# Grouped-query decode attention with an MLP: the query weights in two loads, the output weights in two pieces

## The chip, the cores and the metric

The kernel runs on one core of one Trainium2 chip. The metric is the device time of one execution in microseconds; the kernel before has a median of 1303.21 us over three runs.

## What is computed

One token goes through a layer norm; the normed row feeds an attention block with a cached key and value, and beside it a two-layer MLP; the sum of both and of the input is the output. All is float32.

```
x  = A_x                                   # 1 x 512
xn = layernorm(x)
q  = (xn @ wq) -> 32 heads of 128          # wq 512 x 4096
k, v: 8 heads of 65536 x 128, each shared by 4 query heads
p  = softmax(q k^T * 128**-0.5);  o = p v
out = x + (o -> 4096) @ wo + relu(xn @ w1) @ w2     # wo 4096 x 512, w1 512 x 1792, w2 1792 x 512
```

## The kernel before

The cache is 512 MB and is read once. Keys and values come in 64 chunks of 8 MB (32 of each), 128 rows (one per partition) of 64 KB each; the key chunk goes to the tile `kt`, the value chunk to `vt`, so each of the two is filled again as soon as its reader gives it free. There are four chunk pairs (PARTS) for each of 8 key heads.

The order is written out by hand on each engine, with named semaphores.

SyncE (SP) issues all the large loads, on one queue. First the query weights `wq` into `kt`, in the pieces of WQ_CUTS (floats per row; L151 for the first, L159 for the rest), then w1 into `wt` (L160), then key and value chunks in turn, each after the semaphore that frees its tile (L161 to L170). Behind the last value chunk come the output weights `wo` into `kt`, in the pieces of WO_CUTS (L171 to L173; a slice is 512 floats, 2 KB of a row, and there are 32), and, after `hT` is there, w2 into `wt` in five pieces (L175 to L177). The output is stored at L179.

TensorE (PE) turns through one loop NCH + 2 = 34 times (L270 to L322). The back half of each turn is "scores": eight rounds of 2048 columns of `kt`, four matmuls each (eight recorded passes each, since they are float32), against the padded query tile `qpad` (L307 to L320). Turn 0 uses it for `xn @ wq`, turns 1 to 32 for the key chunks, turn 33 for `o @ wo`: this is why both weights go to `kt`. Ahead of the rounds PE takes two semaphores: `q` (qpad is written) and `k` (16 counts of a landed load). The front half of a turn (from turn 2) is the maximum, the MLP's first product, probabilities times values (L292) and the row sums (L299, L302). Behind the last turn PE does w2 (L331, L339), the sum over the heads' parts (L328 with `yd`, L352 with `ysum`).

VectorE (DVE) transposes the scores out of PSUM, two rounds at a time into `tr` (turn_scores, L361 to L368), and raises `free` for PE behind each. PE's rounds 6 and 7 take four counts of `free`. In turns 0 and 33 the names in `gates` put a wait for a load into two of these four steps: a drain behind the transpose that waits for the load's 16 counts, and only then raises `free`. So rounds that read a later piece wait for that piece by way of DVE. In turn 33 DVE then reduces to yT, spreads it to `yd` (L409), adds `ysum` (L413) and transposes the result (L417).

GpSimd (POOL) finishes the layer norm (L208 to L212), takes `ends` (the landing of the first piece of wq), writes `xn` into `qpad` and raises `q` (L213, L214); later it does the MLP's first product's scaling (L219 to L224) and `hT` (L226).

The semaphores of wq's three pieces are `ends`, `k` and `wq2`; those of wo's three pieces `k`, `wo1` and `wo2`.

```
WQ_CUTS = [4096, 4096, 8192]
WQ_SEMS = ["ends", "k", "wq2"]
WO_CUTS = [16, 8, 8]
...
take(pe, sem("q"))
take(pe, sem("k"), 16)
for s in range(ROUNDS):
```

Of the kernel before, what the change touches and what calls it, by code (L numbers as in the profile page):

```python
# [37 lines left out]
XA = D // P  # L38
WIDE = 4
ROUNDS = 8  # L40
WQ_CUTS = [4096, 4096, 8192]
WQ_SEMS = ["ends", "k", "wq2"]
WO_CUTS = [16, 8, 8]
W2_CUTS = [6, 4, 2, 1, 1]
W2_SUM = 12
W2_ROWS = 10
# [3 lines left out]
def take(e, sem, n=1):  # L50

    return e.sem_inc(sem, -n).wait_op(sem, n, "sem-ge")  # L52


def starts(cuts):
    return [sum(cuts[:i]) for i in range(len(cuts) + 1)]
# [3 lines left out]
def attention_and_mlp_kernel(  # L60
# [12 lines left out]
    sp, pe, dve, act, pool = nc.sync, nc.tensor, nc.vector, nc.scalar, nc.gpsimd  # L73
# [7 lines left out]
    def sem(name):  # L81
        if name not in sems:
            sems[name] = nc.alloc_semaphore(name)
        return sems[name]

    def after(ins, name, n=1):

        return ins.wait_op(sem(name), n, "sem-ge")
# [53 lines left out]
    v_row = v[0].rearrange("(n p b) d -> n p (b d)", p=P, b=NB)  # L142
    wq_at, wo_at, w2_at = starts(WQ_CUTS), starts(WO_CUTS), starts(W2_CUTS)

# [5 lines left out]

    load = sp.dma_start(kt[:, : WQ_CUTS[0]], wq_row[:, : WQ_CUTS[0]]).then_inc(sem(WQ_SEMS[0]), 16)  # L151
    tc.no_tile_sem_insts.add(load.ins.name)
# [3 lines left out]
    inside = section.enter_context(tc.tile_critical(sync_engine=mybir.EngineType.Pool, no_gpsimd_drain=True))  # L156
    for i in range(1, len(WQ_CUTS)):
        cut = slice(wq_at[i], wq_at[i + 1])
        sp.dma_start(kt[:, cut], wq_row[:, cut]).then_inc(sem(WQ_SEMS[i]), 16)  # L159
    sp.dma_start(wt, w1_row).then_inc(sem("w1"), 16)  # L160
# [9 lines left out]
    take(sp, sem("kfree"))  # L170
    for i in range(len(WO_CUTS)):  # L171
        cut = slice(wo_at[i] * D, wo_at[i + 1] * D)
# [11 lines left out]
    def link(ins):  # L184

        if chain[0]:
            after(ins, "pool", chain[0])
        chain[0] += 1
        return ins.then_inc(sem("pool"), 1)
# [21 lines left out]
    link(pool.tensor_mul(st[:, 7:8], st[:, 5:6], st[:, 6:7]))  # L211
    link(pool.tensor_scalar_mul(xn, xc, st[:, 7:8]))  # L212
    take(pool, sem("ends"), 16)  # L213
    after(pool.tensor_copy(qpad[:, :XA], xn), "pool", chain[0]).then_inc(sem("q"), 1)  # L214
    f = DFF_ALL
    w1_of = [wt[:, a * f : (a + 1) * f] for a in range(XA)]
# [144 lines left out]
    def turn_scores(gates=(), free=None):  # L361

        for s in range(ROUNDS // 2):
            if free and s == ROUNDS // 2 - 1:
                after(dve.nop(), "p2d", s + 1).then_inc(sem(free), 1)
            ins = after(dve.transpose(tr2[:, s * 1024 : (s + 1) * 1024], pair[s % 2]), "p2d", s + 1)  # L366
            if s < len(gates):
                ins = after(dve.drain(), gates[s], 16)  # L368
            ins.then_inc(sem("free"), 1)

    dve.memset(ones, 1.0)
    dve.memset(banks, 0.0).then_inc(sem("zero"), 1)
    after(dve.reciprocal(st[:, 5:6], st[:, 4:5]), "ln", 3).then_inc(sem("ln"), 1)
    turn_scores(["wq2", "wq2"], free="kfree")
    dve.drain()
    dve.tensor_reduce(qall, of_own_row(NQ, XA), axis=AX.X, op=ALU.add).then_inc(sem("dve"), 1)
    take(dve, sem("p2d"), 4)
    take(dve, sem("dve"))
    with dve.Fori(0, HEADS) as h:
        dve.tensor_copy(qpad[:, :GROUP], qall[:, bass.ds(h * GROUP, GROUP)]).then_inc(sem("q"), PARTS)  # L380
        with dve.Fori(0, PARTS):
            turn_scores()
            dve.drain()
            dve.reduce_max(m, tr.rearrange("p b i -> p i b")[:, :GROUP, :], axis=AX.X).then_inc(sem("d2p"), 1)  # L384
            after(dve.reduce_max(mg, pma[:GROUP, :P], axis=AX.X), "p2d", 5).then_inc(sem("dve"), 1)
            after(
                dve.tensor_scalar(dg, ident[:GROUP, :GROUP], mg, -scale, op0=ALU.mult, op1=ALU.mult), "dve", 1  # L387
            ).then_inc(sem("d2p"), 1)
            after(dve.tensor_tensor(nb_new, pmb[:, :GROUP], nb_run, op=ALU.min), "p2d", 6).then_inc(sem("dve"), 1)
            after(dve.tensor_sub(diff, nb_new, nb_run), "dve", 2).then_inc(sem("dve"), 1)  # L390
            after(dve.tensor_copy(nb_run, nb_new), "dve", 3).then_inc(sem("bias"), 1)
            after(dve.tensor_copy(o_sb.rearrange("p b d -> p (b d)"), acc), "p2d", 7).then_inc(sem("d2p"), 1)  # L392
            dve.tensor_mul(lo_run, lo_run, corr).then_inc(sem("dve"), 1)
            take(dve, sem("p2d"), 8)
            after(dve.tensor_add(lo_run, lo_run, lo_new), "dve", 4).then_inc(sem("dve"), 1)  # L395
            take(dve, sem("dve"), 5)
        dve.reciprocal(diff, lo_run[:, 0, :]).then_inc(sem("dve"), 1)
        dve.memset(nb_run, 3.0e38)
        after(
            dve.tensor_mul(oT[:, bass.ds(h * GROUP, GROUP)], lo_run[:, 1, :], diff), "dve"  # L400
        ).then_inc(sem("dve"), 1)
        take(dve, sem("dve"), 2)
    dve.tensor_copy(qpad, oT).then_inc(sem("q"), 1)
    dve.transpose(ysum[:, : FB * 32], hrow).then_inc(sem("hx"), 1)  # L404
    turn_scores(["wo1", "wo2"])
    dve.drain()
    dve.tensor_reduce(yT, of_own_row(CT, NQ), axis=AX.X, op=ALU.add).then_inc(sem("dve"), 1)
    after(
# [2 lines left out]
        ), "dve",  # L411
    ).then_inc(sem("yd"), 1)
    after(dve.tensor_add(ysum, y4, x4), "p2d", 5).then_inc(sem("ysum"), 1)  # L413
    for _ in range(3):
        dve.drain()
    after(
        dve.transpose(ysb.rearrange("p i a -> p a i"), yacc.rearrange("p (e a) -> p a e", a=CT)), "p2d", 6  # L417
# [38 lines left out]
```

## Time and profile before

| | us |
|---|---|
| median of 3 runs (1303.2 to 1303.97) | 1303.21 |
| span of the profiled execution | 1301.3 |
| PE busy | 774.9 |
| DVE busy | 274.8 |
| ACT busy | 76.2 |
| POOL busy | 34.8 |
| HBM read | 560.99 MB, 431 GB/s over the span |

The profiled execution's span runs from its first to its last instruction; the median of the runs is 1.9 us longer, and that rest lies outside the span. Shares of busy time are averages: what counts for this change is the first 25 us and the last 35 us, so the timeline of these two stretches is read, with the issue and the landing of the loads.

### The profile page before, as it was taken

The page shows a single profiled execution, that of the slowest core. Times are in us where ns is not written, and L with a number is a line of the kernel's source. Part 1 is how long each engine was busy: PE and PEld are TensorE (multiplying, and loading weights), DVE is VectorE, ACT ScalarE, POOL GpSimd, SP SyncE. Part 2 cuts the span into 40 slices and gives each one's busy share as a digit, 9 for nine tenths or more (in the row PEclk, how much of TensorE's full clock was granted, in tenths as well). Part 3 has the DMA queues.
Part 4 walks back from the last instruction along what each step waited for, and adds up shares of the span by engine and source line. Part 5 has one row for each costly group of instructions (what it writes and reads, how often), then busy time and mean ns, then how long its engine had stood idle before and what let it go on. Part 6 is the DMA issues. An engine that isn't in the chain of part 4 may idle for free.

```text
span 1301.3 us, 13055 instructions
## 1 busy us (share of the span) xinstructions
PE 774.9 (60%) x5474; PEld 231.1 (18%) x5474; DVE 274.8 (21%) x466; ACT 76.2 (6%) x299; POOL 34.8 (3%) x30
## 2 busy tenths in 40 slices
PE   3365674665576456566555566666567466557557
PEld 1111121111121111121111121111112111112112
DVE  2211222211222220222220122221122221122222
ACT  1000000000000000000000000000000000000000
POOL 1900000000000000000000000000000000000000
PEclk9677877776887777786776777677777777777779
DMA  9999999999999999999999999999999999999998
GB/s 403 451 419 451 419 451 419 435 435 419 451 419 451 419 451 419 449 421 423 447 419 451 419 451 419 451 419 435 435 419 451 419 451 419 451 419 443 427 420 370
DMA packets 11236, 561.02 MB, mean 431 GB/s; under 512 B 1505, under 2 KB 1505, under 8 KB 1890
## 3 DMA queue, kind: packets, MB, share of 16 engines
q1 hardware_dynamic: 11088, 561.00, 99.7%
q10 hardware_dynamic: 146, 0.00, 0.0%
q8 instruction: 1, 0.02, 0.0%
q14 instruction: 1, 0.01, 0.0%
HBM read 560.99 MB, written 0.00 MB: 431 GB/s over the span
## 4 chain that ended last, share of the span: by engine, by line
issue 94%; DMA 3%; POOL 2%; SPq 0%; PE 0%; DVE 0%; POOLq 0%
DMA wt<-w 3%; POOL wt L219 1%; POOL wt L224 0%; POOL wt L222 0%; POOL wt L223 0%; SPq L177 0%; SPq L159 0%; PE banks L339 0%; DVE ysb L417 0%; SPq L151 0%; POOL hT L226 0%; SPq L452 0%; POOLq L156 0%
## 5 line engine op out<-in xcount | busy, mean ns | idle before, releaser
L313 PE MATMUL banks<-kt,qpad 128*32 128x512 f32 x2176 | 310.0, 733 | 311.1 <-PEq L52 308.7
L292 PE MATMUL banks<-vt,probs 128*16 128x512 f32 x2048 | 271.3, 690 | 82.1 <-PEq L52 82.1
L366 DVE STREAM_TRANSPOSE tr<-banks 128x1024 f32<-128x1024 f32 x136 | 170.0, 1250 | 471.4 <-PE banks L313 466.8
L313 PEld LDWEIGHTS banks<-kt,qpad 128*32 128x32 f32 x2176 | 84.5, 131 | 509.6 <-issue 496.3
L281 PE MATMUL banks<-wt,ones 128*1 128x448 f32 x768 | 121.3, 786 | 0.0
L292 PEld LDWEIGHTS banks<-vt,probs 128*16 128x16 f32 x2048 | 68.4, 108 | 298.4 <-issue 298.4
L392 DVE COPY o_sb<-banks 128x512 f32<-128x512 f32 x32 | 22.1, 692 | 455.3 <-PE banks L292 455.3
L254 ACT ACTIVATE corr<-diff 128x8 f32<-128x8 f32 x32 | 6.7, 208 | 1179.8 <-ACTq L52 1179.8
L256 ACT ACTIVATE probs<-tr,nb_new 128x128 f32<-128x128 f32 x128 | 65.3, 521 | 0.0
L276 PE MATMUL banks<-ident,m 128*4 128x128 f32 x32 | 9.7, 303 | 78.9 <-DVE m L384 78.9
L302 PE MATMUL banks<-sel,o_sb 128*128 128x4 f32 x256 | 32.8, 252 | 18.7 <-PEq L52 18.7
L302 PEld LDWEIGHTS banks<-sel,o_sb 128*128 128x128 f32 x256 | 31.0, 191 | 20.6 <-issue 20.6
L226 POOL TENSOR_SCALAR hT<-ysum 128x14 f32<-128x14 f32 x1 | 0.3, 257 | 1220.7 <-DVE ysum L404 1220.7
L384 DVE TENSOR_REDUCE m<-tr 128x4 f32<-128x512 f32 x32 | 32.2, 1006 | 2.9
L281 PEld LDWEIGHTS banks<-wt,ones 128*1 128x1 f32 x768 | 20.2, 100 | 58.9 <-issue 58.4
L277 PE MATMUL banks<-dg,ones 4*128 4x4 f32 x64 | 15.4, 309 | 20.0 <-DVE dg L387 20.0
L256 ACT ACTIVATION_READ_ACCUMULATOR probs<-tr,nb_new 128x1 f32 x128 | 24.0, 187 | 0.0
L276 PEld LDWEIGHTS banks<-ident,m 128*4 128x4 f32 x32 | 2.6, 81 | 108.0 <-DVE m L384 108.0
L219 POOL TENSOR_SCALAR wt<-wt,xn 128x1792 f32<-128x1792 f32 x4 | 19.1, 4797 | 16.5 <-DMA wt<-w 16.5
L277 PEld LDWEIGHTS banks<-dg,ones 4*128 4x128 f32 x64 | 12.6, 245 | 27.1 <-DVE dg L387 27.1
L299 PEld LDWEIGHTS banks<-part_sum,ones 128*128 128x128 f32 x64 | 9.5, 188 | 27.2 <-issue 27.2
L395 DVE TENSOR_TENSOR lo_run<-lo_run,banks 128x8 f32<-128x8 f32 x32 | 5.2, 163 | 40.0 <-DVEq L52 40.0
(69 smaller groups left out, 91.1 us busy)
## 6 DMA issues: line engine op xcount, KB each, us to landing
kt<-wq SPq DMA_DIRECT2D x2, 2048.0 KB, 9.3
kt<-wq SPq DMA_DIRECT2D x1, 4096.0 KB, 20.8
kt<-wo SPq DMA_DIRECT2D x1, 4096.0 KB, 15.5
kt<-wo SPq DMA_DIRECT2D x2, 2048.0 KB, 22.2
wt<-w SPq DMA_DIRECT2D x1, 3584.0 KB, 28.9
wt<-w SPq DMA_DIRECT2D x1, 1536.0 KB, 9.5
wt<-w SPq DMA_DIRECT2D x1, 1024.0 KB, 11.7
kt<-k SPq DMA_DIRECT2D x32, 24.1
```

What stands on the lines that cost most here:

```text
L219: last = pool.tensor_scalar_mul(w1_of[a], w1_of[a], xn[:, a : a + 1])
L256: last = act.activation(probs[:, :, g], tr[:, :, g], AF.Exp, bias=nb_new[:, g : g + 1], scale=scale, accum_out=part_sum[:, g : g + 1],)
L276: after(pe.transpose(pma[:GROUP, :P], m, ident), "d2p").then_inc(sem("p2d"), 1)
L277: after(pe.matmul(pmb[:, :GROUP], ones[:GROUP, :], dg, start=True, stop=True), "d2p", 2).then_inc(sem("p2d"), 1)
L281: ins = pe.matmul(hrow[32 * c : 32 * c + 1, :], ones[:, :1], hb[:, :, 32 * c : 32 * c + 32], start=True, stop=True,)
L292: last = pe.matmul(acc[c : c + WIDE * GROUP, :], probs[:, b : b + WIDE, :].rearrange("p b g -> p (b g)"), vt[:, b * DH : (b + WIDE) * DH], ...
L299: pe.matmul(lo_new[:, 0, :], ones, part_sum, start=True, stop=True).then_inc(sem("vfree"), 1)
L302: last = pe.matmul(lo_new[:, 1, :], o_sb[:, b, :], sel[:, b, :], start=(b == 0), stop=(b == WIDE - 1),)
L313: last = pe.matmul(pair[s // 2 % 2][32 * c : 32 * c + 32, s % 2 * 512 : s % 2 * 512 + 512], qpad, kb[:, s * 16 : s * 16 + 16, c, :], start ...
L366: ins = after(dve.transpose(tr2[:, s * 1024 : (s + 1) * 1024], pair[s % 2]), "p2d", s + 1)
L384: dve.reduce_max(m, tr.rearrange("p b i -> p i b")[:, :GROUP, :], axis=AX.X).then_inc(sem("d2p"), 1)
L392: after(dve.tensor_copy(o_sb.rearrange("p b d -> p (b d)"), acc), "p2d", 7).then_inc(sem("d2p"), 1)
```

## The change

wq comes in two loads of 32 KB rows (8192 floats) where it came in three of 16, 16 and 32 KB. The first raises `ends`; the piece that raised `k` is gone, so POOL adds 16 to `k` right after it has taken `ends`. wo comes in two pieces, 24 and 8 slices (48 KB and 16 KB rows) where it came in three of 16, 8 and 8. Its first piece raises `k`, its second `wo1`. Six of the eight rounds of turn 33 read the first piece, so DVE's first gate in that turn is empty and the second one waits for `wo1`. DVE loses one drain there and gets one ahead of its last transpose (four, not three).

```
-WQ_CUTS = [4096, 4096, 8192]
-WQ_SEMS = ["ends", "k", "wq2"]
-WO_CUTS = [16, 8, 8]
+WQ_CUTS = [8192, 8192]
+WQ_SEMS = ["ends", "wq2"]
+WO_CUTS = [24, 8]
...
     take(pool, sem("ends"), 16)
+    pool.sem_inc(sem("k"), 16)
...
-            if s < len(gates):
+            if s < len(gates) and gates[s]:
                 ins = after(dve.drain(), gates[s], 16)
...
-    turn_scores(["wo1", "wo2"])
+    turn_scores([None, "wo1"])
...
-    for _ in range(3):
+    for _ in range(4):
         dve.drain()
```

On SP's queue at the end of the program (`vt<-v` is the last value chunk, `kt<-wo` the output weights, `wt<-w` the pieces of w2; the shape is partitions x floats) stands before:

```order
L163 COMPARE_AND_BRANCH
L169 DMA vt<-v 128x16384
L173 DMA kt<-wo 128x8192
L173 DMA kt<-wo 128x4096 x2
L177 DMA wt<-w 128x3072
L177 DMA wt<-w 128x2048
```

and now:

```order
L163 COMPARE_AND_BRANCH
L169 DMA vt<-v 128x16384
L173 DMA kt<-wo 128x12288
L173 DMA kt<-wo 128x4096
L177 DMA wt<-w 128x3072
L177 DMA wt<-w 128x2048
```

The middle piece has become part of the first, and PE's take of `k` in turn 33 now covers 24 slices, not 16.

On DVE in the same turn (`tr<-banks` is a transpose of two rounds' scores; p2d is PE's count of finished rounds) the waits stand before:

```order
L403 COPY qpad<-oT 128x32
L404 STREAM_TRANSPOSE ysum<-banks 128x448
L366 STREAM_TRANSPOSE tr<-banks 128x1024 [waits p2d]
L366 STREAM_TRANSPOSE tr<-banks 128x1024 [waits wo1,p2d]
L366 STREAM_TRANSPOSE tr<-banks 128x1024 [waits wo2,p2d]
L366 STREAM_TRANSPOSE tr<-banks 128x1024 [waits p2d]
L407 TENSOR_REDUCE yT<-tr 128x4
```

and now:

```order
L404 COPY qpad<-oT 128x32
L405 STREAM_TRANSPOSE ysum<-banks 128x448
L367 STREAM_TRANSPOSE tr<-banks 128x1024 [waits p2d] x2
L367 STREAM_TRANSPOSE tr<-banks 128x1024 [waits wo1,p2d]
L367 STREAM_TRANSPOSE tr<-banks 128x1024 [waits p2d]
L408 TENSOR_REDUCE yT<-tr 128x4
L410 TENSOR_TENSOR yd<-ident,yT 128x512 [waits dve]
```

The wait behind the first transpose is gone, and the one behind the second is for the load of the last 8 slices, as it was (it is called wo1 now).

## Rows read from the trace of the kernel before

**Rows 1.** The page's head, and its DMA queue: packets, MB, share of 16 engines.

```profile
span 1301.3 us, 13055 instructions
q1 hardware_dynamic: 11088, 561.00, 99.7%
```

**Rows 2.** DMA issues of wq, the first piece, then lines L159's two: us to landing.

```profile
kt<-wq SPq DMA_DIRECT2D x1, 2048.0 KB, 7.2
...
L159 SPq DMA_DIRECT2D kt<-wq x2: 334/386/439, 1.3 to 1.7; - x2
...
DMA to landing us min/median/max: 11.5/16.1/20.8
```

**Rows 3.** Timeline of the first 25 us: start, us, engine, line, operation, [idle before <-releaser].

```profile
14.15 0.31 POOL L212 TENSOR_SCALAR xn<-xc,st 128x4 f32<-128x4 f32 x1
14.52 0.19 POOL L214 COPY qpad<-xn 128x4 f32<-128x4 f32 x1
15.00 5.17 PE L313 MATMUL banks<-kt,qpad 128*32 128x512 f32 x32 [3.03 <-PEq L52]
22.66 1.25 DVE L366 STREAM_TRANSPOSE tr<-banks 128x1024 f32<-128x1024 f32 x1 [2.90 <-DMA kt<-wq]
```

**Rows 4.** Timeline of PE: the scores of the first and the last key chunk.

```profile
50.77 9.48 PE L313 MATMUL banks<-kt,qpad 128*32 128x512 f32 x64 [24.50 <-PEq L52]
...
1250.46 8.68 PE L313 MATMUL banks<-kt,qpad 128*32 128x512 f32 x64 [7.62 <-PEq L52]
```

**Rows 5.** Line L173 alone, the issues of wo: first and last start, us to landing.

```profile
L173 SPq DMA_DIRECT2D kt<-wo x3: 338/424/426, 1263.9 to 1264.8; - x3
...
DMA to landing us min/median/max: 15.5/20.0/24.4
```

**Rows 6.** Timeline of the end, PE and DVE, from the last row sums.

```profile
1279.94 1.03 PE L302 MATMUL banks<-sel,o_sb 128*128 128x4 f32 x8 [0.59 <-PEq L52]
1282.74 5.36 PE L313 MATMUL banks<-kt,qpad 128*32 128x512 f32 x48 [1.77 <-PEq L52]
...
1289.33 1.25 DVE L366 STREAM_TRANSPOSE tr<-banks 128x1024 f32<-128x1024 f32 x1 [1.64 <-DMA kt<-wo]
1289.39 1.92 PE L313 MATMUL banks<-kt,qpad 128*32 128x512 f32 x16 [1.29 <-PEq L52]
...
1291.37 1.25 DVE L366 STREAM_TRANSPOSE tr<-banks 128x1024 f32<-128x1024 f32 x1 [0.79 <-PE banks L313]
...
1293.13 0.69 DVE L409 TENSOR_TENSOR yd<-ident,yT 128x512 f32<-128x512 f32 x1
...
1295.44 1.09 PE L331 MATMUL banks<-wt,hT 128*1 128x512 f32 x8
1296.59 0.69 DVE L413 TENSOR_TENSOR ysum<-banks,x 128x512 f32<-128x512 f32 x1 [2.77 <-PE banks L331]
...
1298.02 0.40 PE L339 MATMUL banks<-wt,hT 128*1 128x128 f32 x8
```

**Rows 7.** The chain that ended last, its last landing: start, us.

```profile
1285.18 12.80 DMA wt<-w
```

**Rows 8.** Timeline of PE: five of the 32 value products, by the idle time before.

```profile
147.31 8.76 PE L292 MATMUL banks<-vt,probs 128*16 128x512 f32 x64 [3.45 <-PEq L52]
...
186.02 7.06 PE L292 MATMUL banks<-vt,probs 128*16 128x512 f32 x64 [1.16 <-PEq L52]
...
611.80 8.85 PE L292 MATMUL banks<-vt,probs 128*16 128x512 f32 x64 [0.81 <-PEq L52]
...
1231.11 9.80 PE L292 MATMUL banks<-vt,probs 128*16 128x512 f32 x64 [3.99 <-PEq L52]
...
1269.82 9.22 PE L292 MATMUL banks<-vt,probs 128*16 128x512 f32 x64 [3.45 <-PEq L52]
```

**Rows 9.** Stretches: us; PE, PEld, DVE, ACT, POOL busy (instructions); granted clock; DMA share; GB/s.

```profile
1250.46:1253.74 3.28, 3.28 (x16) 0.88 (x20) 0.00 (x0) 0.00 (x0) 0.00 (x0) 0.50 0.74 320
...
1282.74:1288.20 5.46, 5.36 (x48) 1.69 (x48) 2.76 (x3) 0.00 (x0) 0.26 (x1) 1.00 1.01 432
```

## The prediction

> **What bounds the kernel now.** I read the head of the page and its DMA queue first, then the issues and landings, then the timeline of the two ends, where the change lies. SP's queue is busy for 99.7% of 16 engines over the whole span of 1301.3 us, with 561.00 MB [rows 1]. So the engines behind it wait, and a matmul saved in the loop is worth nothing. The pace of the stream comes from PE's scores, which start as a key chunk lands: the first at 50.77, the last at 1250.46 [rows 4], 31 pairs of chunks in 1199.69 us, 38.70 us for 16.78 MB or 433.5 GB/s; one chunk of 8.39 MB takes 19.35 us. The last transfer of the program is w2, issued at 1285.18 and landed 12.80 us later, at 1297.98 [rows 7]; PE's last eight passes start at 1298.02 [rows 6]. So the end is set by the landing of the last byte, with a tail of some 3 us behind it, and beside it by a chain of PE and DVE steps that only just keeps up. The change can act in two ways: on the length of the stream (fewer loads), and on that chain at the end, where PE now waits for a larger piece.
>
> **Part 1, wq in two loads.** The first piece landed 7.2 us after its issue, and the second, issued at 1.34, 11.5 us after it, at 12.8 [rows 2]. The new first load has the bytes of both, so it lands at about 12.8 as well (the stream is the same). POOL has the layer norm done at 14.15 + 0.31 = 14.46 and writes qpad at 14.52 [rows 3], so its take of `ends` is met 1.6 us before it gets there, as before. The added increment on POOL has no row; between the end of L212 and the start of L214 lie 0.06 us that hold a take of the same kind, so I bound it by 0 and 0.06 us and take 0.05. Behind it are queued the copy to qpad and POOL's w1 work, which waits for w1 until 31 us. PE starts its first rounds 0.05 us later at worst; these end at 15.00 + 5.17 = 20.17, and DVE then waits 2.90 us for the last piece of wq, until 22.66 [rows 3]. That cover of 2.5 us hides it. Without the cover it would cost the same 0.05 us. Price on the path: 0.
>
> **Part 2, the stream.** Two loads fewer, out of 77: 128 rows and 16 semaphore writes less for each, 288 packets of 11088 [rows 1], with the same bytes. What a load costs beyond its bytes is bounded from rows: wo's third piece, issued at 1264.8, landed 24.4 us later, at 1289.2 [rows 5], and the last value chunk had landed before its product started at 1269.82 [rows 8]. Three loads with 8.39 MB thus took 19.3 to 19.4 us, where one load of the same bytes takes 19.35. The second piece of wq took (1.34 + 11.5) - (0.73 + 7.2) = 4.91 us [rows 2] for 2.10 MB that at the stream's pace want 4.84. So 0 to 0.1 us a load, and below nothing I exclude, since no byte is added and no load waits for another engine anew. Two loads: 0 to 0.2 us, and I take 0.1 us off the landing of everything behind.
>
> **Part 3, wo in pieces of 24 and 8.** Here the change adds a wait. PE takes `k` before its first round. Before, `k` came from the 16 slices, landed at 1263.90 + 15.5 = 1279.4 [rows 5], and the query tile (`q`) came later, so PE started at 1282.74 [rows 6]. Now `k` comes with 24 slices, which land when the second piece did: 1264.33 + 20.0 = 1284.3 [rows 5]. PE starts at about 1284.4 (0.1 for the semaphore), 1.65 us later, and its idle time, since L302 ended at 1279.94 + 1.03 = 1280.97, grows from 1.77 to 3.4 us. Queued behind on PE is all that is left of the program; DVE waits for PE's rounds.
>
> How long do the rounds take? Before, 48 passes ran from 1282.74 and then PE stood until 1289.39 for the last eight slices; the last 16 passes took 1.92 us, to 1291.31, and DVE's last transpose started at 1291.37 [rows 6]. Now the last slices are there at 1289.1, before PE needs them, so 64 passes run without a stop. At full clock 64 passes take 7.06 us [rows 8]: 1284.4 + 7.06 = 1291.46, a delay of only 0.15 us. PE gets its wait back from the stop that it no longer has.
>
> But the clock. The 48 passes now run at a granted clock of 1.00 [rows 9], the 2.4 GHz level, behind an idle time of 1.77 us. After 7.62 us of idleness the key scores began at 0.50, 1.2 GHz, 16 passes in 3.28 us [rows 4, 9]. Nearest to 3.4 us are the value products: two that stood idle for 3.45 us took 8.76 and 9.22 us, one with 3.99 took 9.80, and one with 1.16 took the 7.06 [rows 8]. All 16 products behind 3.44 us or more lost 1.70 us or more. A short wait is no guarantee: six behind 0.81 to 0.99 us were slow too, as the one of 8.85 us [rows 8], since there the clock had fallen earlier. So the loss is 1.70 to 2.16 us at my gap, 2.74 at most in this table, 0 if the clock stays up. I take 1.9, by the two nearest rows: rounds end at 1293.35, DVE's last transpose starts at 1293.4, 2.05 us late.
>
> The Trainium skill, "TensorE: Matmul & The Clock Gate", section "Part 1: The HAM clock gate", says that the default state is throttled and that activity releases it, on a count that runs free of the kernel. The rows on idle time agree with the first; by the second, the same wait could cost different amounts in different runs, which no row here shows for this place.
>
> What of these 2.05 us reaches the end? `yd` was done at 1293.13 + 0.69 = 1293.82 [rows 6], now 1295.87. PE has six rows of w2 done by then (12 passes, 1.3 us, from 1293.35). The passes with `yd` take 0.2 to 1.0 us, and I take 0.45; the eight passes of w2's second piece, which started at 1295.44 on its landing and took 1.09 us [rows 6], now end at 1295.87 + 0.45 + 1.09 = 1297.4. DVE's `ysum` starts at 1297.45 where it was 1296.59. It takes 0.69, so L352 starts at 1298.2, and three sets of eight passes at 0.40 each (L352, and the last two pieces of w2, long landed; the last eight of before took as much) end at 1299.4, where the last ended at 1298.42. The end is 1.0 us later: half of the delay goes into the wait for w2's landings that stood there before. Bounds: with a loss of 1.70 and 0.2 us for `yd`, 0.5 us; with 2.74 and 1.0, 2.4 us.
>
> **Part 4, drains on DVE.** One goes, one comes. Between the end of DVE's last score transpose (1291.37 + 1.25 = 1292.62) and its reduce 0.1 us pass with a drain in them, so 0 to 0.1 us. The new one stands behind `ysum`, while PE does 1.2 us of passes: hidden. Ahead of the final transpose it would show in full, 0.1.
>
> **Sum.** -0.1 for the stream, which also moves wo's landing and so the chain, +1.0 for the chain: +0.9 on a span of 1301.3. The median of the runs lies 1.9 us over that span; I let that rest stand. 1303.21 + 0.9 = 1304.1.
>
> **The rivals.**
> A. The clock stays up: PE's delay is 0.15 us, the wait for w2 takes it, and the stream's 0.1 us is left: 1303.1. For it: 1.77 us of idleness left the clock alone, and L302 is activity just before. Against: the two rows at 3.45 us.
> B. Slower, by a clock that stays low through all of turn 33. At 1.2 GHz a pass takes 3.28 / 16 = 0.205 us [rows 9], 64 take 13.1, 6.1 more than at full clock; the chain then passes the extra on in full, (6.1 - 1.9) beyond my +0.9: 1308.3. It gives more than 2.6 us from a loss of some 3.6 us, 38 slow passes. Against: the largest loss in the rows is 2.74.
> C. Faster: a load pays a start of its own. The first load took 7.2 us for bytes that want 4.84 [rows 2], 2.4 us more. If each did, two fewer would save 4.7 us: 1298.5, and 1299.5 with the chain's loss. Against: three loads took as long as one in part 2, since they stand in the queue ahead of time. The Trainium skill, "DMA: Bandwidth & Descriptors", section "Anatomy of one DMA", gives a fit of 2.0 us plus bytes at 436 GB/s for each DMA (for the other kind of queue): by it two loads are 4 us and the time 1299.2. The trace disagrees: one chunk of 8.39 MB would take an estimated 21.2 us by it, and takes 19.35.
> D. Nothing moves, because another load's landing is what PE waits for anyway: that is A's time.
>
> **How the numbers follow.** Forecast 0.76, A and D together 0.17, B 0.05, C 0.02. About 0.2%, 2.6 us, is what a measurement of this kernel can tell from no change. The forecast with its bounds (1303.6 to 1305.5) and A lie within that, so same is 0.93, slower 0.05, faster 0.02. The range leaves out B, C and the outermost of the forecast: 1302.9 at A less 0.2, to 1305.4.
>
> **What would show it.** Right: PE's rounds in turn 33 start within 0.3 us of 1284.4 behind some 3.4 us of idle time; the first 16 or more passes at a granted clock of 0.50; no stop before the last 16; `ysum` about 0.9 us later; the last w2 landing 0.0 to 0.2 us earlier; PE idle no longer on w2 before its last passes. Wrong: a granted clock of 1.00 there (A), 38 slow passes or more (B), landings of wq or wo that move by over 1 us (C), or DVE's wait for wq2 gone in turn 0.

## The result, and the profile after

The changed kernel has a median of 1305.58 us (1304.35 to 1307.76), the kernel before, on the same chips, 1303.52 (1303.06 to 1304.15): 2.06 us more, a ratio of 1.0017 with a 95% interval of 1.0011 to 1.0023. It is slower, by less than the 0.2% that I had set as the bound, and above the range that I gave (1302.9 to 1305.4). The runs of the kernel before lie within 1.1 us, those of the changed one within 3.4: that spread is a finding of its own.

The execution profiled took 1306.53 us, 0.95 more than the median. Its page (head, DMA queue, and the chain that ended last, by engine) answers [rows 1, 7]:

```profile
span 1304.8 us, 13054 instructions
...
q1 hardware_dynamic: 10800, 561.00, 99.5%
...
PE 1%; DVE 0%; issue 0%; DVEq 0%
```

The 288 packets are gone. The chain that ended last no longer goes back to a landing of w2: it is PE and DVE from 1286.4, where PE's wait for wo's first piece ends, to 1302.5.

The start, in the timelines of ACT, POOL, PE and SP (start, us, engine, line, operation, [idle before <-releaser]), against [rows 3, 4]:

```profile
14.28 0.21 ACT L241 ACTIVATE xc<-xT 128x4 f32<-128x4 f32 x1 [11.03 <-DMA xT<-x]
...
19.53 0.19 POOL L215 COPY qpad<-xn 128x4 f32<-128x4 f32 x1
...
20.02 9.55 PE L314 MATMUL banks<-kt,qpad 128*32 128x512 f32 x64 [3.04 <-PEq L52]
...
29.76 0.33 SPq L162 DMA_DIRECT2D kt<-k  x1
...
52.21 8.82 PE L314 MATMUL banks<-kt,qpad 128*32 128x512 f32 x64 [22.64 <-PEq L52]
```

In the kernel before, ACT and SP stood so:

```profile
9.27 0.21 ACT L240 ACTIVATE xc<-xT 128x4 f32<-128x4 f32 x1 [6.03 <-DMA xT<-x]
...
26.46 0.33 SPq L162 DMA_DIRECT2D kt<-k  x1
```

The first row is the surprise. The layer norm starts 5 us late because `x`, 2 KB on ACT's queue, landed late. Its issue, in the list of DMA issues of the kernel before (KB, us to landing):

```profile
xT<-x ACTq DMA_DIRECT2D x1, 2.0 KB, 8.2
```

and in that of the changed one, with w1's:

```profile
wt<-w SPq DMA_DIRECT2D x1, 3584.0 KB, 29.4
...
xT<-x ACTq DMA_DIRECT2D x1, 2.0 KB, 13.2
```

So POOL wrote qpad at 19.53 (before 14.52), PE's first rounds began at 20.02 (15.00), and all eight rounds ran in one go, 64 passes in 9.55 us, partly at the low clock: the first 24 take 5.07 us, 0.21 us a pass, which is the pace of the 0.50 stretch in [rows 9], and the other 40 take 4.48. (The column of the granted clock reads 1.00 for all of it, because the profile's first record of the clock is its rise at 25.06.) `kt` came free at 29.6, and SP issued the first key chunk at 29.76, where it was 26.46. That chunk landed 22.0 us after its issue, at 51.8 (before 50.4, 24.0 us after). A load that stands in the queue ahead of time takes 19.35 us; this one was issued when w1, which landed at 31.2 (29.4 after its issue at 1.73), had 1.4 us to go, and the chunk landed 20.6 us behind w1. The stream lost about 1.3 us there, and all that follows is late by it.

The end, in the timelines of PE and DVE, against [rows 6]:

```profile
1279.85 1.03 PE L303 MATMUL banks<-sel,o_sb 128*128 128x4 f32 x8 [0.58 <-PEq L52]
1286.43 9.52 PE L314 MATMUL banks<-kt,qpad 128*32 128x512 f32 x64 [5.56 <-PEq L52]
...
1296.01 1.25 DVE L367 STREAM_TRANSPOSE tr<-banks 128x1024 f32<-128x1024 f32 x1 [0.47 <-PE banks L314]
...
1298.51 0.59 PE L329 MATMUL banks<-yd,ones 128*1 128x512 f32 x1 [0.85 <-DVE yd L410]
...
1300.44 0.69 DVE L414 TENSOR_TENSOR ysum<-banks,x 128x512 f32<-128x512 f32 x1 [1.99 <-PE banks L332]
...
1301.41 0.62 PE L340 MATMUL banks<-wt,hT 128*1 128x128 f32 x16
```

PE waits 5.56 us for wo's first piece (the stream is 2.0 us late by then, and the wait for 24 slices comes on top), the clock falls, and the 64 passes take 9.52 us. The stretches show it (us; busy times; granted clock; DMA):

```profile
1286.43:1291.00 4.57, 4.57 (x24) 1.33 (x28) 0.87 (x1) 0.00 (x0) 0.00 (x0) 0.50 1.02 434
1291.00:1295.90 4.90, 4.90 (x48) 1.37 (x44) 2.88 (x3) 0.00 (x0) 0.00 (x0) 0.96 0.98 412
```

PE's last passes end at 1302.03 (before 1298.42), though w2 had landed at 1299.9 (1297.98): of these 3.6 us, 2.0 are the stream and 1.6 the chain at the end. The gap behind w1 is 1.3 of the stream's 2.0; most of the rest is in three loads of the first 250 us, of which more under "Left open".

### The profile page after: what moved, and what is told of

It reads as the page before. It is cut to its first block, busy times and chain, and to the rows that moved or that the text cites. A ratio compares the mean times of both kernels' runs of the same rounds, so it can differ in the third digit from the quotient of the medians.

```text
span 1304.8 us, 13054 instructions
## 1 busy us (share of the span) xinstructions
PE 772.4 (59%) x5474; PEld 231.3 (18%) x5474; DVE 278.9 (21%) x466; ACT 76.1 (6%) x299; POOL 34.8 (3%) x30
## 5 line engine op out<-in xcount | busy, mean ns | idle before, releaser
L303 PEld LDWEIGHTS banks<-sel,o_sb 128*128 128x128 f32 x256 | 31.0, 191 | 20.6 <-issue 20.6
L278 PEld LDWEIGHTS banks<-dg,ones 4*128 4x128 f32 x64 | 12.0, 233 | 27.1 <-DVE dg L388 27.1
## 6 DMA issues: line engine op xcount, KB each, us to landing
wt<-w SPq DMA_DIRECT2D x1, 3584.0 KB, 29.4
```

Of the source, the lines that this page charges most:

```text
L278: after(pe.matmul(pmb[:, :GROUP], ones[:GROUP, :], dg, start=True, stop=True), "d2p", 2).then_inc(sem("p2d"), 1)
L303: last = pe.matmul(lo_new[:, 1, :], o_sb[:, b, :], sel[:, b, :], start=(b == 0), stop=(b == WIDE - 1),)
```

## The experiments

The theory from these profiles, X: the loss is mainly in the start; x's rows take turns with wq's rows on the DMA engines, larger rows make x late, and x makes the first key chunk late. The rivals: W, all of it is wo's larger piece; S, the stream is slowed by the larger rows or the fewer loads themselves.

### One part at a time

The wq part alone (WQ_CUTS, WQ_SEMS and POOL's increment).

> The wq part alone (two loads of 32 KB rows, GpSimd passes the landing on); wo stays in 16, 8 and 8. Theory X (x's load, on another queue, takes turns with wq's rows on the DMA engines, so it lands 5 us later, and the first key chunk is issued too late to follow w1 without a gap): x lands 13.2 us after its issue, the first key chunk is issued at 28.5 to 30.5, it lands 1.3 us or more later than before, and the time is 1.3 to 2.0 us over the kernel before. Rival W (all of the loss is PE's wait for wo's larger piece and the lower clock behind it): the time is within 0.3 us of the kernel before.

1305.3 us, the kernel before on the same chip 1303.45: 1.85 us more (ratio 1.0014, 1.0005 to 1.0023). Its PE timeline, and its first key chunk on SP:

```profile
19.94 9.65 PE L314 MATMUL banks<-kt,qpad 128*32 128x512 f32 x64 [3.03 <-PEq L52]
...
29.78 0.33 SPq L162 DMA_DIRECT2D kt<-k  x1
...
1294.00 1.88 PE L332 MATMUL banks<-wt,hT 128*1 128x512 f32 x12 [1.62 <-DMA wt<-w]
```

x landed 13.1 us after its issue, and PE began the first key chunk at 52.07, 1.3 us late. The profiled execution, 1304.03 us, is the fastest of the eleven, so the trace accounts for 1.3 us and not for all of the 1.85. At the end PE waits for w2 as it did before. W falls: by the medians, the part that I had priced at nothing carries most of the loss.

The wo part alone (WO_CUTS, the gates, the drain).

> The wo part alone (24 and 8 slices, one wait fewer on VectorE); wq stays in three loads. Theory X: x lands 8.2 us after its issue, the first key chunk is issued at 26.5, no gap in the stream; what is left is the wait of 3.4 us and the low clock in turn 33, 0.5 to 1.2 us over the kernel before. Rival W: 2 us over it.

1304.06 us, 0.6 more (1.0006, 0.9997 to 1.0015: by the time alone not clear of no change). SP issued the first key chunk at 26.54 and PE began it at 50.79. The end, PE and DVE:

```profile
1284.42 8.63 PE L313 MATMUL banks<-kt,qpad 128*32 128x512 f32 x64 [3.85 <-PEq L52]
...
1293.12 1.25 DVE L366 STREAM_TRANSPOSE tr<-banks 128x1024 f32<-128x1024 f32 x1 [0.47 <-PE banks L313]
...
1295.62 0.59 PE L328 MATMUL banks<-yd,ones 128*1 128x512 f32 x1 [0.82 <-DVE yd L409]
...
1297.55 0.69 DVE L413 TENSOR_TENSOR ysum<-banks,x 128x512 f32<-128x512 f32 x1 [1.99 <-PE banks L331]
1298.30 0.40 PE L352 MATMUL banks<-ysum,ones 128*1 128x128 f32 x8 [0.36 <-DVE ysum L413]
1298.51 0.62 PE L339 MATMUL banks<-wt,hT 128*1 128x128 f32 x16
```

This is the forecast's case, row by row: PE's end is at 1299.13, 0.7 us late.

### Is it x?

wq in one load of 64 KB rows: the dose is doubled once more (the lines are against the changed kernel; wo is put back to three pieces).

```
-WQ_CUTS = [8192, 8192]
-WQ_SEMS = ["ends", "wq2"]
+WQ_CUTS = [16384]
+WQ_SEMS = ["ends"]
...
-    turn_scores(["wq2", "wq2"], free="kfree")
+    turn_scores(free="kfree")
```

> wq in one load of 64 KB rows (no wait for a second piece on VectorE; GpSimd passes its landing on); wo as before. x has 8 rows on each DMA engine. Theory X: each of them waits for one row of wq, so the landing grows by 5.0 us when the row doubles from 16 to 32 KB (8.2 to 13.2 us seen) and by 10 more from 32 to 64 KB: x lands some 23 us after its issue, PE's first scores start near 30, the first key chunk is issued at 37 to 40.5 and lands 9 to 12 us later than before; the time is 9 to 12 us over the kernel before. If the 13 us of the changed kernel have another cause (a fixed delay): x lands at 13 to 14, and the time is at most 3 us over the kernel before.

1313.19 us (two runs) against 1303.4, 9.8 more. The layer norm's first step on ACT, PE's first rounds and the first key chunk on SP:

```profile
22.95 0.21 ACT L241 ACTIVATE xc<-xT 128x4 f32<-128x4 f32 x1 [19.71 <-DMA xT<-x]
...
28.69 8.84 PE L314 MATMUL banks<-kt,qpad 128*32 128x512 f32 x64 [3.04 <-PEq L52]
...
37.72 0.33 SPq L162 DMA_DIRECT2D kt<-k  x1
```

The line of that chunk's issue alone, its landing:

```profile
DMA to landing us min/median/max: 22.0/22.0/22.0
```

x landed 21.9 us after its issue. With rows of 16, 32 and 64 KB beside it: 8.2, 13.2, 21.9. x has 128 rows, eight for each of 16 engines; 16 KB at one engine's share of the stream's pace take 16384 x 16 / 433.5e3 = 0.60 us. If each row of x waits for one row of wq, 16 KB more in a row are 4.8 us more and 32 KB more 9.7; the steps are 5.0 and 8.7. That is about one row for each. The three landings alone would also fit another reading, that x waits until the first load of wq is through (landed at 7.9, 12.9 and 22.7; x at 9.2, 14.2 and 22.8). The packets decide it: q1 is SP's queue, q10 ACT's. In the kernel before, the DMA queues from 4.0 to 5.2 us hold

```profile
q1 hardware_dynamic: 32, 0.52, 103.0%
q10 hardware_dynamic: 32, 0.00, 1.5%
```

two rows of each for each of 16 engines, and in the changed kernel from 5.4 to 6.6 us, as long a stretch,

```profile
q1 hardware_dynamic: 16, 0.52, 101.1%
q10 hardware_dynamic: 16, 0.00, 0.8%
```

one row of each. So x goes row by row, one of its rows behind each row of wq. The Trainium skill, "DMA: Bandwidth & Descriptors", section "Queues, rings and completion order", says that an engine takes turns between the queues it has work for, a packet of typically 9 to 17 descriptors at a time. The runs agree on the turns and not on their size: here a turn holds one row of x, and eight rows in one turn would have been held up once.

The key chunk again landed 22.0 us after its issue. Where the queue has run dry a load needs 2.6 us more than its 19.35, and to leave no gap the first key chunk has to be issued by about 31.1 - 2.6 = 28.5. The kernel before did so at 26.46, with 2 us to spare. (The last kernel below, with both repairs, tries the limit: issued at 28.63, 2.9 us ahead of w1's landing at 31.5, its first key chunk landed at 50.9, 19.35 us behind w1, without a gap.)

x late by itself. A first try put four table loads ahead of x's issue on ACT:

```
+    for _ in range(2):
+        act.preload_act_table(AF.Exp)
+        act.preload_act_table(AF.Sqrt)
     act.dma_start(xT, x.rearrange("(p a) -> p a", p=P)).then_inc(sem("x"), 16)
```

> The kernel before with four table loads on ScalarE ahead of its load of x, so that x is issued about 5 us later; wq stays in three loads and wo in three pieces. Theory X: the lateness of x alone is enough: first scores near 20, the first key chunk issued at 28.5 to 30.5, and 1.3 to 2.5 us over the kernel before, as the wq part alone (+1.85). Rival S (the larger rows themselves): the time of the kernel before, within 0.3 us.

1303.31 us, the time of the kernel before (1303.4). It didn't do what it should: the trace has x issued at 1.07, since the table loads don't hold the issue. They had ended at 7.4 when the layer norm still waited for x:

```profile
10.59 0.20 ACT L243 ACTIVATE xc<-xT 128x4 f32<-128x4 f32 x1 [3.18 <-DMA xT<-x]
```

x landed 9.4 us after its issue, 1.2 us more than before; why, the runs don't show. PE's first rounds began at 16.33 and still ended before wq's last piece: the cover that the prediction named is real, and holds 1.3 us. So x was held by a semaphore:

```
+    act.wait_ge(sem("zero"), 1)
     act.dma_start(xT, x.rearrange("(p a) -> p a", p=P)).then_inc(sem("x"), 16)
```

> The kernel before, with ScalarE's load of x held until VectorE has cleared PSUM (5.6 us); wq stays in three loads and wo in three pieces. Theory X: the lateness of x alone is enough. x is issued near 5.7 and lands near 14, PE's first scores start near 20, the first key chunk is issued at 28.5 to 30.5 and lands about 21.9 us after its issue, 0.8 to 2 us late; the time is 1.0 to 2.0 us over the kernel before. Rival S (wq's larger rows or fewer loads slow the stream themselves): within 0.3 us of the kernel before.

1305.52 us, 2.06 more than 1303.46 (1.0018, 1.0009 to 1.0027). PE and SP:

```profile
22.04 9.12 PE L314 MATMUL banks<-kt,qpad 128*32 128x512 f32 x64 [3.03 <-PEq L52]
...
31.36 0.33 SPq L162 DMA_DIRECT2D kt<-k  x1
...
53.57 8.72 PE L314 MATMUL banks<-kt,qpad 128*32 128x512 f32 x64 [22.41 <-PEq L52]
```

x came 2 us later than meant (issued at 5.62, landed 10.6 us after), so the first key chunk was issued at 31.36 and landed 21.8 us later. wq stands in its three old loads here. S isn't needed: lateness of x is enough.

The changed kernel with x ahead of wq on SP's queue:

```
+    xload = sp.dma_start(xT, x.rearrange("(p a) -> p a", p=P)).then_inc(sem("x"), 16)
     load = sp.dma_start(kt[:, : WQ_CUTS[0]], wq_row[:, : WQ_CUTS[0]]).then_inc(sem(WQ_SEMS[0]), 16)
...
-    act.dma_start(xT, x.rearrange("(p a) -> p a", p=P)).then_inc(sem("x"), 16)
```

> The changed kernel with the load of x issued on SyncE's queue, ahead of wq, not on ScalarE's. Theory X: x lands within 4 us, the first key chunk is issued by 27.5 and follows w1 without a gap; the first issue moves wq back by some 0.5 us, so the time is that of the wo part alone plus 0.5, 1.0 to 1.7 us over the kernel before. Rival S (the larger rows or the fewer loads themselves slow the stream, not x): 2 us or more over the kernel before, plus 0.5, as the stream is as late as in the changed kernel.

1304.88 us, 1.43 more (1.0013, 1.0004 to 1.0022), 0.8 over the wo part alone, with runs from 1303.69 to 1307.17. SP and PE:

```profile
26.94 0.33 SPq L165 DMA_DIRECT2D kt<-k  x1
...
51.02 9.15 PE L316 MATMUL banks<-kt,qpad 128*32 128x512 f32 x64 [24.27 <-PEq L52]
```

x landed 1.7 us after its issue, the first key chunk was issued at 26.94, and PE began it at 51.02, 0.25 late: the gap is gone, with the larger rows and the fewer loads still there, so S falls by the trace. The time by itself doesn't tell 1.4 from 2.1 us, since the intervals overlap; the trace does, but for its own execution, the fastest of the eleven. Why the median lies 1.2 us above that one is not shown.

### Is it the clock, in the wo part?

PE's wait filled with matmuls of ones into PSUM that nobody reads, between its two takes, in every turn:

```
         take(pe, sem("q"))
+        for i in range(12):
+            c = 32 * (i % CT)
+            pe.matmul(
+                pmb[c : c + 1, 128:512], ones[:, :1], ones.unsqueeze(1).to_broadcast([P, 3, P]),
+                start=True, stop=True,
+            )
         take(pe, sem("k"), 16)
```

> The wo part alone, with 12 matmuls of ones (384 columns, one output row each, into PSUM that nobody reads) between PE's take of q and its take of k in every turn, so that PE isn't idle ahead of wo's rounds. If the low clock is the cost of the wo part: the 64 passes of turn 33 take about 7.1 us at a granted clock of 1.00, and the time is within 0.3 us of the kernel before, 0.5 us or more under the wo part alone. If the wait for the larger piece itself is the cost: the same time as the wo part alone.

1306.26 us, 2.8 more, with runs from 1303.91 to 1309.45: neither of the two. In the profiled run, the fastest of the six, turn 33 did what it should (64 passes in 7.05 us, and PE then waiting for w2). PE at the end:

```profile
1285.71 7.05 PE L319 MATMUL banks<-kt,qpad 128*32 128x512 f32 x64
...
1298.63 0.79 PE L345 MATMUL banks<-wt,hT 128*1 128x128 f32 x16
```

PE's last passes end at 1299.42, 0.44 us behind w2's last landing at 1298.97. That is the tail of the kernel before (1298.42 behind 1297.98); in the wo part alone it is 1.2 us (1299.13 behind 1297.93). But the stream is late: wq's last piece landed 1.3 us late, and the DMA queues in the stretch from 19 to 20 us hold a packet that no other kernel so far had there:

```profile
q8 instruction: 1, 0.02, 6.0%
```

It is 16 KB of program code, on one DMA engine for 0.06 x 16 = 0.96 us, and the loads share the 16 engines. Every kernel here has one such packet close to its end, the kernel before at 1297.97; this one has a second, among the loads of the start. The Trainium skill, "Runtime: NRT & Kernel Launch", section "Instruction fetch mechanics", says that an engine's program is fetched in blocks of 16 KiB, and that a branch out of what is at hand stalls it; the size agrees. The same matmuls behind the row sums, not in the first two turns:

```
             last.then_inc(sem("p2d"), 1)
+            for i in range(18):
+                c = 32 * (i % CT)
+                pe.matmul(...)
         take(pe, sem("q"))
```

> The wo part alone, with 18 matmuls of ones behind the last row sums of every turn from the third on, not in the first two turns, so that the start of the program is untouched. PE has work until about 1284.2 in turn 33. If the low clock is the cost of the wo part: 64 passes in about 7.1 us, the end on w2's last landing, and a time within 0.3 us of the kernel before, 0.4 us or more under the wo part alone (+0.6). If activity of PE itself disturbs the stream (e4 was 2.8 us over the kernel before at the median): over the wo part alone.

1305.59 us, 2.2 more, from 1304.55 to 1309.75. Again a packet of code, now at 16.0 us, and wq's last piece 1.5 us late. PE's second half of turn 0 then stood idle for 3.05 us and took 6.54 us for 32 passes (3.64 before), so the first key chunk was issued at 30.91. In turn 33, 64 passes took 7.07 us, and PE's last passes ended 0.44 us behind w2's last landing (1300.85 and 1300.41), again the tail of the kernel before. A longer program was the next thing to take away: a loop, with fewer instructions.

```
             last.then_inc(sem("p2d"), 1)
+            with pe.Fori(0, 4):
+                for c in range(CT):
+                    pe.matmul(...)
         take(pe, sem("q"))
```

> The wo part alone with the same idle-filling matmuls of ones behind the row sums of every turn from the third on, written as a loop of four times four, so that PE's program grows by some 10 instructions and not by 36 to 60. If it was a load of PE's program code on one DMA engine (at 16.0 and 19.5 us in the two longer kernels) that made them slow: no such load before the end, wq lands as before, 64 passes in about 7.1 us, and the time within 0.3 us of the kernel before. If PE's activity disturbs the stream: 2 us over the kernel before, as with those two.

1305.83 us, 2.4 more, but from 1305.39 to 1306.05 only: the smallest spread of the kernels with the wo part. PE at the end:

```profile
1284.49 7.07 PE L319 MATMUL banks<-kt,qpad 128*32 128x512 f32 x64 [2.87 <-PEq L52]
1292.99 1.88 PE L337 MATMUL banks<-wt,hT 128*1 128x512 f32 x12 [1.43 <-DMA wt<-w]
...
1297.39 0.40 PE L358 MATMUL banks<-ysum,ones 128*1 128x128 f32 x8
1297.60 0.40 PE L345 MATMUL banks<-wt,hT 128*1 128x128 f32 x7
1300.65 0.80 PE L345 MATMUL banks<-wt,hT 128*1 128x128 f32 x9 [2.65 <-issue]
```

The DMA queues from 1298 to 1299:

```profile
q8 instruction: 1, 0.02, 5.8%
```

The start is clean and turn 33 runs at full clock; PE waits for w2's landings again, and up to 1297.6 all is where it was before ([rows 6] and 1297.98 for the last landing). Then PE stands for 2.65 us in the midst of its last passes, waiting for nothing that the trace shows, while 16 KB of code are fetched. Without this stop the span would be 1304.1 - 2.65 = 1301.45, that of the kernel before (1301.3). So the clock is the cost of the wo part: with it up, the two kernels without a stop have the old tail, and this one has it up to the stop. The repair put another cost in its place. That the fetch causes the stop is read from their times, not tried by itself, and the fetch alone doesn't make one: the kernel before has its fetch at 1297.97, beside its last passes, and no stop.

Both repairs, x ahead on SP's queue and this loop, on the changed kernel:

> The changed kernel with both repairs: x loaded ahead of wq on SyncE's queue, and the loop of matmuls that fills PE's idle time. If x and the clock are the whole cost: 0.3 to 0.6 us over the kernel before (SyncE's extra issue at the start, some 0.45 us, less 0.1 for the two loads). If something else in the change costs: 1 us or more over it.

1306.28 us, 2.8 more, from 1305.96 to 1312.42: by its time the expectation fails. There is again a stop, of 2.66 us, in the same place (the span of the profile was 1304.2). By the trace, without it, 1301.5, 0.2 over the kernel before, near the 0.3 to 0.6 expected. That is a subtraction: only the two kernels with the loop have the stop, and the kernel before with the loop alone was not run. By the time, no version here beats the kernel before.

### Why do its runs differ?

The changed kernel once more:

> The changed kernel once more, for where its executions differ. Theory X with the clock: the start loses 1.3 us plus what the clock of the wq scores adds (its 64 passes take 7.1 to 10.5 us by where they fall), and the end 0.5 to 2.4 us more; the stream between is the same within 0.3 us. In the first profile three loads of the first 250 us were 0.2 to 0.3 us longer than the rest; by this theory that has no part in it and doesn't come again.

1306.97 us. x landed 13.6 us after its issue, wq's 64 passes took 9.52, the first key chunk was issued at 30.13 and PE began it at 53.29, 2.5 us late; turn 33's took 9.42 behind 5.56 us of idleness. The end costs what it cost in the first profile. The start costs 1.1 us more: the key chunk landed 22.7 us after its issue here, and w1 0.5 us late. Why they did is not shown, and with it the spread of the runs stays open. It isn't the gap alone: the kernel with x ahead of wq, whose profile has no gap, spreads over 3.5 us as well.

## Why the prediction was wrong, point by point

**What bounds the kernel** was right: the stream, with a chain at the end that only just keeps up.

**Part 1, wq, priced at 0, is the step that failed.** It cost 1.85 us alone, 1.3 of them in its trace as a late first key chunk. The increment on POOL and the landing of wq's first 4 MB are as worked out (0.73 + 12.2 = 12.9; 12.8 was expected). The error lies in the layer norm's "done at 14.46", which I carried over as a constant. It hangs on x, a load on another queue that I did not cost, though the edit changes the rows that it shares the engines with. And the cover that I named, 2.5 us until wq's last piece, was the cover for PE's first rounds; the one that decided is SP's, the first key chunk in the queue before w1 ends, 2 us. A late x eats the first, then the second. So Part 2's "no load waits for another engine anew" is wrong as well: the first key chunk waits longer for PE's scores.

The clock has a part in this too. The late wq scores run in one go, 9.55 us for 64 passes where 7.06 is full clock [rows 8]. At full clock `kt` would have been free 2.5 us earlier, near 27.1, and by the 28.5 worked out above there would be no gap; this is worked out, not tried.

**Part 2, the stream**: -0.1 us was set, and in the wo part alone wo and w2 landed within 0.1 us of before. Too small to be seen.

**Part 3, wo**: the mechanism and its steps were right, the size somewhat too large. PE started at 1284.42 (1284.4 expected), 64 passes took 8.63, a loss of 1.57 (1.9 forecast; it lies under the lower bound of 1.70), `ysum` was 1.0 us late (0.86), PE's end 0.7 (1.0); the median moved by 0.6. Its 0.6 is not clear of noise; the trace is what bears it. In the full change this chain is longer, because the late stream adds 2.0 us to PE's wait (5.56, not 3.4).

**Part 4, the drains**: nothing to see. In the wo part alone DVE's reduce starts 0.08 us behind the last score transpose and its final transpose 0.07 us behind PE's last passes, in the kernel before 0.10 and 0.07.

**The sum**: 1.85 and 0.6 make 2.45, the whole 2.06; the intervals of the parts are wider than that difference. Instead of +0.9 it was +2.06.

**The rivals**: A, no fall of the clock, was not seen at this place. What I gave for it, that 1.77 us of idle time left the clock alone, was luck of that one profile: in the kernels with wq in one load and with x late, 48 passes behind the same 1.77 us took 7.94 to 8.25 us where they took 5.36, at no cost, since wo's last piece wasn't there yet. B, low clock all through, was not seen either (24 slow passes at most in the kernels with the larger piece). C is refuted by the -0.1: with one load less, the wo part alone has the same landings. In the full change wo landed 2.0 us later, more than the 1 us that I had set as C's sign, and the other way. The slower side had a mechanism of its own that stood in none of them. The range failed by 0.2 us, since every case shared the same price for part 1.

**Left open**: between its first key chunk and its last value chunk the changed kernel's profile has 1271.89 - 52.21 = 1219.68 us, the kernel before 1219.05 [rows 4, 8], and the wq part alone 1270.90 - 52.07 = 1218.83. The changed kernel once more has 1272.42 - 53.29 = 1219.13, so it doesn't come with every execution. In the first profile it is three loads of the first 250 us that landed 19.5 to 19.6 us behind the one before them, where the others take 19.35. The expectation was that they don't come again; two of 19.5 did. Loads as long as that are in five of the six profiles with a gap behind w1 and in none of the seven without one. What makes them long was not found.

## What to carry to other kernels

A small load isn't small when its rows take turns with large ones: before rows are made larger, list every load that is in flight beside them, on any queue, and who waits for it. For a kernel that its stream bounds, the number to guard is how long before the end of one load the next is issued, here 2.6 us at least; an edit that touches anything ahead of that issue, a layer norm or a clock, is costed against it. And a matmul that fills a wait is program code: it can put a code fetch among the loads, and in the two kernels with the loop it came with a stop of PE in the last passes.

## What the runs showed of the hardware

A load of 2 KB in 128 rows took 8.2, 13.2 and 21.9 us beside rows of 16, 32 and 64 KB, and 1.7 us ahead of them in the same queue; beside them, one of its rows went for each row of the other queue. A load of 8.39 MB issued to a queue that runs dry needs 21.8 to 22.0 us (22.7 in one run) for what takes 19.35 in a full one. Four table loads ahead of an issue on ACT don't delay the issue (1.07 us, 0.98 without them).

A fetch of 16 KB of code holds a DMA engine for 0.93 to 1.31 us. In the two kernels that had one among the loads of the start, wq's last piece landed 1.3 and 1.5 us late. All 13 profiles have one near the end; beside it PE stood for 2.65 us in the two kernels with the loop, and not in the others.

In the changed kernel DVE's copy to qpad, now beside POOL's products over w1 (its timeline):

```profile
31.80 4.29 DVE L381 COPY qpad<-qall 128x4 f32 x1 [0.34 <-DVEq L52]
```

Before, ahead of them, it took 0.17 us. It ended with POOL's first product (31.26 + 4.80); here nobody waits for it.
